# Two PSUM banks for the last two products, two planner costs, and a new order of all queues, in a one-core attention and Fourier-mixing kernel

## The chip, the cores and the metric

The kernel runs on one core of one Trainium2 chip. A core has five engines that run side by side: TensorE (PE in the profile, with its weight loads as PEld), VectorE (DVE), ScalarE (ACT), GpSimd (POOL) and SyncE (SP). SP issues DMAs only; POOL and ACT issue DMAs beside their own work. The metric is the time of one execution on the device in microseconds; lower is better.

## The reference, cut to what matters

Queries, keys and values have 4 batches, 8 heads, 768 positions and 64 elements a head. Attention is local (96 positions back) with 8 global keys and a bias that falls with distance. Its output, per batch 768 x 512, goes through a Fourier mixing and a two-layer network:

```python
scores = scale * np.matmul(q, k.transpose(0, 1, 3, 2)) + bias      # only where local or global
a = softmax(scores); x = np.matmul(a, v)                            # (B, S, H*D)
mixed = np.real(np.fft.fft(np.fft.fft(x, axis=1), axis=2))
u = x + mixed
un = (u - mean(u)) / np.sqrt(var(u) + 1e-06)
return u + np.maximum(un @ w_ch1, 0.0) @ w_ch2                      # 512 -> 2048 -> 512
```

## The kernel before

All work is written down as small units for PE and small operations for the other engines, and then emitted in an order that is written out by hand, one string for each engine (`ORDER` in class `Plan`). PE's units have a letter for their stream and a number in it:

- A: attention. Turning queries and keys (`trans`), scores (`score`), and probabilities times values (`av`). A45 to A60 are batch 2, A61 to A76 batch 3; A61 is the first score of batch 3, of head pair 12 (pairs are counted through the batches, four to each).
- M: mixing. Products with Fourier tables (`y_unit`, `u_unit`) and the turning of the normalised rows for the first three chunks (`nt_unit`). M16 makes chunk 3, M17 is a table product.
- H: the hidden layer. A chunk is 256 of the 3072 rows, there are 12 of them (0 to 11), and for most chunks eight units `ph_unit` make its hidden values, each from one quarter of w1. H24 is the first unit of chunk 3.
- G: the second layer. For each chunk five units, for the last one (chunk 11, `tail`) six: G55 `p1`, G56 `p45`, G57 `p6`, G58 `half(1)`, G59 `p7`, G60 `half(0)`. Chunk sums save one product in eight (lines 1663 to 1676).

An operation on another engine has the name of the unit that it belongs to with a number behind the dot: A10.0 is the first operation that follows A10, here Vector's division of its result; M16.1 and M16.2 make the normalised rows `un` of chunk 3. Operations that belong to no unit begin with T. Those that come up below:

- T.55, T.56: GpSimd loads two quarters of w1. T.84, T.99: GpSimd copies a mirrored piece of a table product. T.85, T.88, T.124 to T.126, T.172 to T.175: GpSimd copies of values (`v_back`, tile vB). T.92: gather of rows of x of batch 1. T.107, T.112, T.117, T.122: loads of values of batch 2. T.110, T.111, T.119, T.152 to T.155, T.160, T.162, T.163, T.165: loads of queries or keys of one head. M7.17, M12.8: GpSimd's inverse deviations of a chunk (`rstd`).
- T.89, T.90: Scalar's queue writes the two halves of x of batch 1 to DRAM; T.91: SP reads them back.
- T.100, T.101, T.102: SP's DMA transposes of `un` to `unT` of chunks 3, 4 and 5. T.136, T.177, T.182, T.185: SP's DMA transposes of queries or keys of a head pair (T.177: the keys of pair 12). T.205, T.206, T.216, T.217, T.267 to T.269: SP stores results.
- T.209: Vector makes a chunk sum for the second layer. T.77, T.78: Vector's steps of the first batch's fold.

PE runs its units strictly in the written order, and so does each of the other engines with its operations; a late operand holds up everything behind it on that engine. Semaphores are set by the tile framework from the program's reads and writes of tiles. GpSimd's DMAs go to a queue of their own (q0 in the profile), SP's to q1, ACT's to q10; all run on the same 16 DMA engines.

PSUM has eight banks. In the last stage four of them serve the rings `ph` and `pg` (two each); `xx` has the other four (two pairs). A unit names the rings that it may take a bank from, and the plan takes the one that comes free first. In the last chunk G58 and G60 both write into the bank that `p45` took for G56 (tile pgD), one into its upper and one into its lower half. The plan counts the two Vector operations that read them before it calls the bank free:

```python
            D_ = GP[c, "D"] = bank(ring, f"pgD_{c}")
            if tail:
                ring.n = 2
```

The plan's costs (the second number of an entry in `pl.later`) only choose among free banks and set the sequence in which the engines' streams are merged while the program is written out; they are no waits on the chip.

Of the kernel before, what the change touches and what calls it, by code (L numbers as in the profile page):

```python
# [17 lines left out]
class Ring(str):  # L18
# [3 lines left out]
    e = 0.0  # L22


class Plan:
# [214 lines left out]
    def unit_start(self, unit):  # L240
# [7 lines left out]
        if not there:  # L248
# [22 lines left out]
        ),  # L271
        "ACT": (
# [11 lines left out]
        ),  # L284
        "DVE": (
# [13 lines left out]
        ),  # L299
        "POOL": (  # L300
# [5 lines left out]
        ),  # L306
        "SP": (
            "T.6 T.0 T.9 T.127 T.35 T.10 T.133 T.128 T.134 T.206 T.136 T.91 T.130 T.137 T.205 T.100 T.131 T.101 T.176 T.177 T.185 T.182 T.102 T.216 T.34 "
            "T.217 T.140 T.186 T.223 T.183 T.222 T.179 T.149 T.180 T.276 T.150 T.151 T.189 T.233 T.234 T.240 T.239 T.198 T.199 T.200 T.257 T.250 T.256 "
            "T.251 T.269 T.267 T.268 "  # L310
# [73 lines left out]
def kernel(  # L384
# [11 lines left out]
    nc = tc.nc  # L396
# [72 lines left out]
    pl = Plan()  # L469
# [178 lines left out]
    def RA(b):  # L648
        return 2 if b else 0
# [168 lines left out]
    def v_back(b, hp):  # L818
        h = slice(2 * hp, 2 * hp + 2)

        def head(r):
            return v16[b % 2][r, h, 0:1, :].to_broadcast([r.stop - r.start, 2, NS - 2, 66])
        after = VN(b, [hp]) + [("sets",)] + [("avh", b - 1, hp)] * (b > 0)
        rows = (slice(0, 32),)

        def cp(eng):
            eng.tensor_copy(vB[hp], v16[b % 2][:, h, 1:NS - 1, :])  # L827
            for r in rows:
                eng.tensor_copy(vB[hp][r], head(r))
        pl.later([("POOL", 0.6 + 0.6 * len(rows), lambda: cp(nc.gpsimd)), ("DVE", 0.3 + 0.3 * len(rows), lambda: cp(V))], after, 0.0, [("vB", b, hp)], rank=RA(b))  # L830
# [473 lines left out]
    def centre(c):  # L1304
# [26 lines left out]
        pl.later([("POOL", 0.82, rstd)], [("ss", c, 0), ("ss", c, 1)], 0.0, [("rstd", c)], rank=2)  # L1331
# [358 lines left out]
    def pg_units(c):  # L1690
# [6 lines left out]
        def prod(o, lhs, rhs, first, last=True):  # L1697
            for j in range(NK):
                nc.tensor.matmul(o, lhs(j), rhs(j), start=(first and j == 0), stop=(j == NK - 1), skip_group_check=True)  # L1699
# [27 lines left out]
        def p45(start, ring):  # L1727
            D_ = GP[c, "D"] = bank(ring, f"pgD_{c}")
            GP[c, "Dr"] = ring
            if tail:  # L1730
                ring.n = 2
# [45 lines left out]
        def half(x, product):  # L1777
            lo, hi = x * HC, (x + 1) * HC

            def run(start, ring):  # L1780
                D_ = GP[c, "D"]
                product(D_[:, lo:hi])
                e = pl.pe(one_us, start)
                if x == 1:
# [3 lines left out]
                         [("ra", c, 1)], e, [("ob", c, 0, x)], ring=GP[c, "Dr"], rank=0)  # L1788
# [19 lines left out]
        if tail:  # L1808
            PG.append(([("s", c, 4), ("rd", c, 0), ("ord", c)], None, half(0, lambda o: prod(o, a(0, 1), bw(1, 0), True))))
# [204 lines left out]
```

## Time and profile before

| | us |
|---|---|
| three runs | 243.40, 242.51, 245.43 |
| median | 243.4 |
| the profiled execution, its own time | 245.22 |
| its span, first to last instruction | 243.4 |
| TensorE busy in it | 231.1 |
| mean granted TensorE clock | 0.990 |

The span is what the profile's numbers are measured in; the profiled execution took 1.8 us more than its span. Times in the profile count from the span's start. In a row of a timeline the columns are the start, the duration, the engine, the line, the operation, what it writes and reads, the shape and the count; in brackets at the end stands how long the engine was idle before it and who ended that. "SPq" and "ACTq" are DMAs that SP and ACT issue. A row of waits gives the engine and line that waited, whom it waited for, the sum of it, how often, and the longest.

### The profile page before, as it was taken

To read this page: it belongs to the slowest core of one execution; us is meant where nothing else is said; L and a number is where in the kernel's file an instruction comes from. 1 tells how busy PE (TensorE), PEld (TensorE's weight loads), DVE (VectorE), ACT (ScalarE), POOL (GpSimd) and SP (SyncE) were. 2 spreads that over 40 slices of the span, in tenths; PEclk is the share of its full clock that TensorE was granted. 3 is DMA by queue.
4 is the path that set the end of the run, shared out by engine and by line. 5 is a ranking of instruction groups with operands and counts; after the bars stand their busy time and mean duration, and the time that the engine had idled before them with its cause. 6 is when DMAs were issued, how large, how long until landed. Compare 5 with 4: busy or idle time off the path is not lost.

```text
span 243.4 us, 7339 instructions
## 1 busy us (share of the span) xinstructions
PE 231.1 (95%) x3074; PEld 193.7 (80%) x3074; DVE 201.5 (83%) x461; ACT 158.3 (65%) x255; POOL 111.9 (46%) x155
## 2 busy tenths in 40 slices
PE   7699899989999996999999999999999999999992
PEld 3366676588988885789888888898889899888881
DVE  3357896989996888489999898999896899898992
ACT  2299599997868855682456877643957677377400
POOL 8998964878440628887026713510070430000220
PEclk9999999999999998899999999999999999999998
DMA  7999999999999999999999695617576272100413
GB/s 184 168 164 175 195 224 207 197 197 174 126 155 181 147 214 119 156 149 108 156 317 246 105 109 149 148 21 202 170 142 164 57 161 54 36 0 4 172 57 118
DMA packets 103249, 35.46 MB, mean 146 GB/s; under 512 B 91088, under 2 KB 98640, under 8 KB 103216
## 3 DMA queue, kind: packets, MB, share of 16 engines
q0 software_dynamic: 72448, 19.16, 79.2%
q1 hardware_dynamic: 27216, 13.08, 27.0%
q10 hardware_dynamic: 3552, 2.75, 4.4%
q8 instruction: 24, 0.39, 0.7%
q14 instruction: 9, 0.07, 0.1%
HBM read 31.44 MB, written 8.65 MB: 165 GB/s over the span
## 4 chain that ended last, share of the span: by engine, by line
PE 81%; ACT 6%; DVE 5%; DMA 5%; issue 1%; ACTq 0%; DVEq 0%
PE ph L1378 23%; PE pgD L1699 16%; PE pgA L1699 12%; PE phA L1471 4%; PE pav L856 4%; PE py L1139 4%; PE phX L1471 3%; PE pu L1226 3%; DMA unT<-un 3%; DMA u<-in_k_dram 3%; ACT ex L800 2%; PE pt L680 2%; PE sc L771 2%; PE sc L739 2%; PE sc L763 2%; PE pf L1047 2%
## 5 line engine op out<-in xcount | busy, mean ns | idle before, releaser
L1378 PE MATMUL ph<-unT,w 128*128 128x256 f16 x576 | 71.3, 275 | 1.9 <-DMA unT<-un 1.8
L1378 PEld LDWEIGHTS <-w 128*128 128x128 f16 x576 | 55.6, 99 | 9.7 <-DMA unT<-un 2.0
L1383 ACT ACTIVATE hT<-ph 128x512 f16<-128x512 f32 x69 | 40.6, 596 | 30.0 <-PE ph L1378 29.6
L1699 PEld LDWEIGHTS <-hT 128*128 128x128 f16 x352 | 34.0, 98 | 4.0
L1329 POOL TENSOR_SCALAR sm<-sm 128x2 f32<-128x2 f32 x12 | 3.6, 301 | 64.2 <-ACT un L1322 62.3
L797 ACT ACTIVATE er<-sc 128x1024 f16<-128x1024 f32 (+1 forms) x24 | 22.3, 952 | 10.7 <-PE sc L771 8.4
L800 ACT ACTIVATE ex<-sc 128x1024 f16<-128x1024 f32 (+1 forms) x24 | 21.8, 971 | 3.1 <-PE sc L739 3.0
L1717 DVE SCALAR_TENSOR_TENSOR u<-pgA,sm,u 128x256 f32<-128x256 f32 (+1 forms) x36 | 20.4, 566 | 2.5 <-PE pgA L1699 1.9
L1717 DVE SCALAR_TENSOR_TENSOR u<-pgD,sm,u 128x512 f32<-128x512 f32 (+1 forms) x25 | 18.0, 724 | 4.9 <-PE pgD L1699 4.6
L812 DVE TENSOR_TENSOR ex<-er,mk 128x1024 f16<-128x1024 f16 (+1 forms) x24 | 16.3, 689 | 5.2 <-ACT er L797 5.1
L868 DVE TENSOR_TENSOR x<-pav,rc 128x384 f16<-128x384 f32 x32 | 16.7, 553 | 0.7
L1322 ACT ACTIVATE un<-un 128x512 f16<-128x512 f16 x24 | 15.0, 626 | 2.5 <-DMA unT<-un 2.5
L856 PEld LDWEIGHTS <-ex 128*128 128x128 f16 x352 | 13.3, 99 | 3.2 <-issue 1.8
L856 PE MATMUL pav<-v,ex 128*128 128x65 f16 x224 | 13.9, 196 | 1.5 <-DVE x L868 0.9
L569 POOL DMA_DIRECT2D qk<-in_q_dram x16 | 13.6, 859 | 1.2 <-PE pt L680 0.7
L921 POOL DMA_INDIRECT xr<-xd,back x3 | 3.5, 1151 | 22.9 <-DVE ex L812 11.7
L569 POOL DMA_DIRECT2D qk<-in_k_dram x16 | 13.6, 860 | 0.1
L1699 PEld LDWEIGHTS <-sb 128*128 128x128 f16 x128 | 12.2, 98 | 1.7
L1568 POOL DMA_INDIRECT out_dram<-u,back x4 | 4.7, 1180 | 17.0 <-DVE u L1717 16.5
L827 POOL COPY vB<-v 128x528 f16<-128x528 f16 x14 | 9.5, 681 | 5.6 <-DMA v<-in_v_dram 4.6
L1152 ACT ACTIVATE zy<-py 128x1024 f16<-128x1024 f32 (+1 forms) x12 | 10.5, 881 | 2.0 <-PE py L1139 1.5
L1699 PE MATMUL pgD<-tt,hT 128*128 128x256 f16 x88 | 11.4, 273 | 0.0
(209 smaller groups left out, 561.8 us busy)
## 6 DMA issues: line engine op xcount, KB each, us to landing
w<-in_moe_w_ch_dram POOLq DMA_DIRECT2D x8, 512.0 KB, 13.9
out_dram<-u SPq DMA_DIRECT2D x15, 256.0 KB, 5.2
v<-in_v_dram POOLq DMA_DIRECT2D x16, 192.0 KB, 7.7
qk<-in_q_dram POOLq DMA_DIRECT2D x16, 96.0 KB, 5.2
qk<-in_k_dram POOLq DMA_DIRECT2D x16, 96.0 KB, 6.3
xr<-xd SPq DMA_DIRECT2D x3, 512.0 KB, 5.3
xd<-x ACTq DMA_DIRECT2D x2, 768.0 KB, 3.8
ex<-w POOLq DMA_DIRECT2D x3, 512.0 KB, 5.9
```

Source lines behind the costliest of these rows:

```text
L569: nc.gpsimd.dma_start(qk16[n][:, w, :, h], src[b, h0 + h].rearrange("(i m) d -> m i d", m=P))
L797: A(mine(), cut(pa), AF.Exp, 0.0, 0.125)
L800: A(cut(expst[hp][:, :, g * 512:g * 512 + (384 if g == 2 else 512)]), cut(pa), AF.Exp, 0.0, 0.125)
L812: VT(o, mine(), m, op=ALU.mult)
L856: nc.tensor.matmul(o[:, s * 65:(s + 1) * 65], lhsT, w, start=(a == 0), stop=(a == len(ops) - 1), skip_group_check=True)
L868: VT(X[b][:, 3 * (k.start + h):3 * (k.start + h) + 3, 2 * hp * Dh:(2 * hp + 2) * Dh].rearrange("p y (h d) -> p y h d", d=Dh), pv[:, h, :, ...
L1322: A(x, x, AF.Square, accum_out=MV[c][:, a, 2:3])
L1378: nc.tensor.matmul(ph[:, a * CH:(a + 1) * CH].rearrange("p (x m) -> p x m", x=2), W1[0][:, d, jb * P:(jb + 1) * P], UNT[c][:, :, d, :], st ...
L1383: pl.later([("ACT", act(512), lambda: A(dst, ph, AF.Relu)), ("DVE", dve(512), lambda: V.tensor_scalar_max(dst, ph, 0.0))], [], e, [("h", c ...
L1471: nc.tensor.matmul(oo.rearrange("p (x m) -> p x m", m=P) if two else oo, lhs(NF * jp + a, d), rhs[:, d], start=(first and a == 0 and d == ...
L1699: nc.tensor.matmul(o, lhs(j), rhs(j), start=(first and j == 0), stop=(j == NK - 1), skip_group_check=True)
L1717: V.scalar_tensor_tensor(o, x, r(t), acc, op0=ALU.mult, op1=ALU.add)
```

## The change

Three things.

The last product, G60 (`half(0)`), takes a bank of its own from `pg` or `ph` (tile pgE) in place of the lower half of pgD. G58 still uses pgD.

```diff
         def p45(start, ring):
             D_ = GP[c, "D"] = bank(ring, f"pgD_{c}")
             GP[c, "Dr"] = ring
-            if tail:
-                ring.n = 2
...
             def run(start, ring):
-                D_ = GP[c, "D"]
+                D_ = GP[c, "D"] if x else bank(ring, f"pgE_{c}")
                 product(D_[:, lo:hi])
...
                 pl.later([("DVE", dve(HC), lambda: stt(u(0)[:, lo:hi], D_[:, lo:hi], 0, u(0)[:, lo:hi]))],
-                         [("ra", c, 1)], e, [("ob", c, 0, x)], ring=GP[c, "Dr"], rank=0)
+                         [("ra", c, 1)], e, [("ob", c, 0, x)], ring=GP[c, "Dr"] if x else ring, rank=0)
...
-            PG.append(([("s", c, 4), ("rd", c, 0), ("ord", c)], None, half(0, lambda o: prod(o, a(0, 1), bw(1, 0), True))))
+            PG.append(([("s", c, 4), ("rd", c, 0), ("ord", c)], ("pg", "ph"), half(0, lambda o: prod(o, a(0, 1), bw(1, 0), True))))
```

Two costs of the plan are raised: that of GpSimd's copy of values and that of its inverse deviation. The instructions stay the same.

```diff
-        pl.later([("POOL", 0.6 + 0.6 * len(rows), lambda: cp(nc.gpsimd)), ("DVE", 0.3 + 0.3 * len(rows), lambda: cp(V))], after, 0.0, [("vB", b, hp)], rank=RA(b))
+        pl.later([("POOL", 0.75 + 0.75 * len(rows), lambda: cp(nc.gpsimd)), ("DVE", 0.3 + 0.3 * len(rows), lambda: cp(V))], after, 0.0, [("vB", b, hp)], rank=RA(b))
...
-        pl.later([("POOL", 0.82, rstd)], [("ss", c, 0), ("ss", c, 1)], 0.0, [("rstd", c)], rank=2)
+        pl.later([("POOL", 1.0, rstd)], [("ss", c, 0), ("ss", c, 1)], 0.0, [("rstd", c)], rank=2)
```

All five strings of `ORDER` are new. PE has the same 284 units, GpSimd the same 114 operations and SP the same 52. Nine operations go from Vector to Scalar (T.72, M0.0, M3.1, M26.0, H20.0, H42.0, H85.1, H92.1, H108.1) and eight from Scalar to Vector (A6.1, M7.10, M7.12, M8.1, H16.0, H19.0, H43.0, H89.1). Most entries move by one to a few places. The stretches that matter here, one string's part to a line:

```diff
 PE, around A10
-A3 A7 A15 A9 A8 A10 A6 A19 A11 A18 A16 A17 A12 A20 A13 A14 A30 A21 A23 A22
+A3 A8 A15 A9 A10 A7 A6 A20 A19 A11 A18 A16 A17 A13 A14 A12 A30 A21 A23 A22
 PE, around H24
-A53 A51 G7 G6 A45 M16 G8 H21 H18 M17 H23 G10 H22 G9 A56 A54 H24 A57 H29 H31 A52 H26
+G7 A53 A51 G6 M16 A45 H21 G8 H18 M17 H23 H22 A56 G9 A54 A52 G10 H24 H26 A57 H29 H31
 DVE, around A21.0
-A15.0 A10.0 A6.0 A11.0 A16.0 T.70 A17.0 T.75 T.76 T.77 T.78 A21.0
+A15.0 A6.1 A10.0 A6.0 A11.0 T.70 A16.0 A17.0 T.75 T.71 T.76 A21.0
 DVE, around M16.2
-A46.1 T.210 A47.1 H17.0 H20.0 G7.0 A53.1 A51.1 G6.0 M16.0 G8.0 M16.2 T.209 A45.1
+A47.1 H17.0 A46.1 T.209 G7.0 T.210 A53.1 M16.0 G6.0 A51.1 G8.0 M16.2 A45.1
 DVE, around M19.2
-M19.0 G14.0 G13.0 A58.0 T.218 M19.2 T.221 A59.0 M19.1
+M19.0 G14.0 M19.1 G13.0 M19.2 A58.0 T.218 A59.0
 ACT, around T.90
-H14.0 M13.0 T.89 M12.7 M12.6 H9.0 M14.0 T.37 T.90 T.40 M15.0 H13.0
+M13.0 H14.0 M7.15 H12.0 H13.0 T.90 M14.0 T.89 M7.16 M15.0
 POOL, around T.55
-T.57 T.65 T.63 T.54 T.61 T.55 T.56 T.114 T.84 T.62 T.85 T.87
+T.54 T.27 T.87 T.63 T.61 T.57 T.65 T.84 T.85 T.55 T.56 T.86 T.88 T.64 T.62
 POOL, from T.108 on
-T.108 T.121 M7.17 T.117 T.119 T.92 T.111 T.110 T.107 T.99 T.122 T.152 M12.8 T.170 T.112 T.169 T.168 T.126 T.211 T.124 T.153 T.154
-T.160 T.157 T.167 T.164 T.155 M16.5 T.125 T.171 T.162 T.163 T.165
+T.108 T.117 T.119 T.121 M7.17 T.92 T.111 T.110 T.107 T.99 M12.8 T.122 T.153 T.152 T.112 T.211 T.126 T.169 T.124 T.168 T.164 T.167
+T.157 T.162 T.125 T.170 T.154 T.155 T.171 T.163 T.165 M16.5
 SP, from T.100 on
-T.100 T.131 T.101 T.176 T.177 T.185 T.182 T.102 T.216 T.34 T.217 T.140
+T.100 T.131 T.101 T.176 T.177 T.102 T.217 T.216 T.185 T.34 T.182 T.140
 SP, at the end
-T.269 T.267 T.268
+T.267 T.269 T.268
```

More of the change, by code (lines that the diff above doesn't have):

```diff
@@ L262 @@
         "PE": (
[8 rows of a table removed]
[8 rows of a table added]
         ),
         "ACT": (
[11 rows of a table removed]
[11 rows of a table added]
         ),
         "DVE": (
[13 rows of a table removed]
[13 rows of a table added]
         ),
         "POOL": (
[5 rows of a table removed]
[5 rows of a table added]
         ),
         "SP": (
-            "T.6 T.0 T.9 T.127 T.35 T.10 T.133 T.128 T.134 T.206 T.136 T.91 T.130 T.137 T.205 T.100 T.131 T.101 T.176 T.177 T.185 T.182 T.102 T.216 T.34 "
-            "T.217 T.140 T.186 T.223 T.183 T.222 T.179 T.149 T.180 T.276 T.150 T.151 T.189 T.233 T.234 T.240 T.239 T.198 T.199 T.200 T.257 T.250 T.256 "
-            "T.251 T.269 T.267 T.268 "
+            "T.6 T.0 T.9 T.127 T.35 T.133 T.128 T.10 T.134 T.206 T.136 T.91 T.130 T.137 T.205 T.100 T.131 T.101 T.176 T.177 T.102 T.217 T.216 T.185 T.34 "
+            "T.182 T.140 T.186 T.223 T.183 T.222 T.179 T.149 T.180 T.276 T.150 T.151 T.234 T.189 T.233 T.240 T.239 T.198 T.199 T.200 T.257 T.256 T.250 "
+            "T.251 T.267 T.269 T.268 "
         ),
```

74 rows, old and new, of the table ORDER are left out of this document.

## Prediction

> **What bounds the kernel now.** I read the page's shares first, then TensorE's (PE's) list of waits, then the table by windows, and the timelines last.
>
> ```profile
> PE 231.1 (95%) x3074; PEld 193.7 (80%) x3074; DVE 201.5 (83%) x461; ACT 158.3 (65%) x255; POOL 111.9 (46%) x155
> ...
> PE   7699899989999996999999999999999999999992
> ...
> PEclk9999999999999998899999999999999999999998
> ...
> PE 81%; ACT 6%; DVE 5%; DMA 5%; issue 1%; ACTq 0%; DVEq 0%
> ```
>
> TensorE works in 231.1 of 243.4 us, so all idle time on it together is 12.3 us, and most of that lies in the first two slices and in the last one. A new order can win only the rest. The one dent far from the ends is slice 16 (the 6), with two slices of a lower clock from there on. The list of PE's waits gives it a name:
>
> ```profile
> PE ph L1378 <- DMA unT<-un: 1.8, 1, 1.8
> ...
> PE pav L856 <- DVE x L868: 0.9, 1, 0.9
> ...
> PE ptu L1351 <- ACT un L1313: 0.5, 1, 0.5
> ```
>
> ```profile
> 90.00:96.00 6.00, 4.15 (x67) 3.34 (x66) 5.86 (x21) 3.43 (x5) 5.84 (x8) 0.95 1.74 129
> 96.00:102.00 6.00, 6.00 (x76) 4.79 (x74) 2.04 (x5) 3.22 (x7) 4.43 (x8) 0.77 2.11 155
> ```
>
> The wait of 1.85 us is followed by a clock of 0.95 and 0.77: 0.05 x 6 + 0.23 x 6 = 1.68 us of TensorE time lost. From 102 us to the end of the products no PE wait is over 0.1 us. So the kernel is bound by TensorE's work, and this change can touch four things: the early waits, this wait with its slow clock, the tail, and whatever new wait the new queues bring.
>
> **The tail (half, p45: two banks).**
>
> ```profile
> 237.05 1.03 PE L1699 MATMUL pgD<-w,mk 128*128 128x256 f16 x8
> 237.92 1.04 PE L1699 MATMUL pgD<-w,zy 128*128 128x256 f16 x8
> 238.39 0.33 SPq L1819 DMA_DIRECT2D out_dram<-u  x1
> 239.00 0.88 DVE L1717 SCALAR_TENSOR_TENSOR u<-pgD,sm,u 128x256 f32<-128x256 f32 x2 [1.12 <-PE pgD L1699]
> 239.51 0.81 SPq L1813 DMA_DIRECT2D out_dram<-u  x2
> ```
>
> G58 (upper half) starts at 237.05 and G60 (lower half) at 237.92, but Vector's two reads of pgD stand one behind the other from 239.00: the first waits for the second product too, since both write one tile. With G60 in a bank of its own (pgE), the first read can go at 237.05 + 1.03 + 0.05 = 238.1 and is done by 238.6, while G60 still runs. The second starts at 239.0 as now and ends at 239.44 instead of 239.88. Its store follows as now. Gain: one read, 0.88 / 2 = 0.44; SP now sends the first half's store ahead of the row that went at 238.39, which costs nothing unless that row lands last: **0.4**. Below by 0 (if the read still waited), above by 0.44.
>
> **The early queues.** A6.1 (one evacuation of turned queries and keys) goes from Scalar to Vector, ahead of A10.0:
>
> ```profile
> 17.71 1.51 ACT L707 ACTIVATE qkT<-pt 128x1536 f16<-128x1536 f16 x1
> ```
>
> ```profile
> 14.82 0.96 DVE L704 COPY qkT<-pt 128x1536 f16<-128x1536 f16 x1 [1.29 <-PE pt L680]
> ...
> 19.25 0.26 DVE L711 COPY mk<-qkT 128x384 f16<-128x384 f16 x1 [1.64 <-ACT qkT L707]
> ...
> 23.93 0.60 DVE L1014 TENSOR_SCALAR zy<-ww 128x128 f16<-128x128 f16 x2
> ```
>
> Scalar gets 1.51 us, Vector pays 0.96 before A10.0, and A11 on PE waits for A10.0's read of the same tile. Vector's idle 1.64 at 19.25 takes that in, and T.77 and T.78 (from 23.93 to 24.7) go behind A21.0, whose read is what the 0.9 us of PE wait ends on. I count nothing: the ends are 0.9 won and 1.0 lost. The 0.5 at ptu stays, as Scalar has the same work ahead of M7.4.
>
> On GpSimd the loads of two quarters of w1 (T.55, T.56) fall behind T.84, which waits for a copy of Vector's until 40.5, and behind a vB copy:
>
> ```profile
> 33.90 0.75 POOL L1891 DMA_DIRECT2D w<-in_moe_w_ch_dram  x1 [0.23 <-DMA v<-in_v_dram]
> ...
> 40.53 0.19 POOL L1173 COPY rev<-zy 128x2 f16<-128x2 f16 x1 [3.40 <-DVE zy L1154]
> ```
>
> ```profile
> w<-in_moe_w_ch_dram POOLq DMA_DIRECT2D x8, 512.0 KB, 13.9
> ```
>
> They go out at about 43 instead of 34. Their queue is full (13.9 us from issue to landing), and the loads ahead of them carry the same bytes in another sequence, so they land when they land now, well before H3 and H4 (54 to 56 us). Cost 0; if the queue ran dry it is up to 43 + 13.9 - 54 = 3 us.
>
> **The wait before H24.** H24 is the first hidden product of chunk 3 and needs the transposed unT that SP issues as T.100.
>
> ```profile
> 88.39 1.23 SPq L1336 DMA_TRANSPOSE unT<-un  x1
> ...
> 92.40 0.60 PE L771 MATMUL sc<-qkT 64*32 64x128 f16 x36
> ...
> 94.85 1.42 PE L1378 MATMUL ph<-unT,w 128*128 128x256 f16 x8 [1.85 <-DMA unT<-un]
> ```
>
> ```profile
> DMA to landing us min/median/max: 3.0/3.2/6.4
> ```
>
> ```profile
> q0 software_dynamic: 988, 0.13, 247.0%
> ```
>
> The transpose took 6.4 us where the median of its kind is 3.2. The last row is the DMA view of 89.7 to 90.5 us: GpSimd's queue q0 alone moves, SP's queue has no packet, though the transpose was issued at 88.39. So GpSimd's loads push it back. Those loads were issued late, after the gather T.92:
>
> ```profile
> 65.88 0.64 POOL L1329 TENSOR_SCALAR sm<-sm 128x2 f32<-128x2 f32 x1 [3.39 <-ACT un L1322]
> ...
> 67.58 1.08 POOL L545 DMA_DIRECT2D v<-in_v_dram  x1
> 68.67 0.84 POOL L569 DMA_DIRECT2D qk<-in_q_dram  x1
> 80.44 1.25 POOL L921 DMA_INDIRECT xr<-xd,back  x1 [10.93 <-PE ph L1378]
> 81.68 1.75 POOL L569 DMA_DIRECT2D qk<-in_k_dram  x2
> 83.33 1.11 POOL L545 DMA_DIRECT2D v<-in_v_dram  x1
> ```
>
> In the new order T.117 and T.119 (67.58, 68.67) stand ahead of M7.17 (65.88, held 3.39 by Scalar), so they leave some 5 us sooner and no longer run beside Scalar's second write of x; SP's T.136 gets its keys sooner; the read T.91 and the gather T.92 follow by an estimated 2 to 3 us sooner, and the three loads behind T.92 with them. They are then over when T.100 goes out (88.4 to 88.7; Vector has T.209 and G6.0 ahead of M16.2 now, so it is no sooner). At the median, 3.2, unT lands at 91.9, and PE comes to H24 at 93.0 plus A52, moved ahead of it, 0.4. The wait goes: **-1.85**, and the slow clock with it: **-1.68**. Bounds: nothing, or all 3.5.
>
> The Trainium skill, "TensorE: Matmul & The Clock Gate", Part 1, has the clock halve after an idle window of about 3.4 us that runs free. The trace agrees on the half clock but not on the length: 1.85 us of idle were enough here. By that rule a new wait of 2 us would cost its own length only; by the row it may cost 1.7 more.
>
> **What is late next.** Past H24 PE is 3.5 us ahead of this trace, and GpSimd is not. A61, the first score of batch 3, needs T.177, the transposed keys of pair 12:
>
> ```profile
> 98.07 0.62 POOL L827 COPY vB<-v 128x528 f16<-128x528 f16 x1 [1.18 <-DMA v<-in_v_dram]
> ...
> 106.07 1.69 POOL L569 DMA_DIRECT2D qk<-in_k_dram  x2
> ...
> 109.57 0.61 POOL L827 COPY vB<-v 128x528 f16<-128x528 f16 x1
> 110.24 0.62 POOL L829 COPY vB<-v 32x528 f16<-32x528 f16 x1
> ```
>
> ```profile
> 113.32 1.21 SPq L658 DMA_TRANSPOSE qkT<-qk  x1
> ```
>
> ```profile
> qkT<-qk SPq DMA_TRANSPOSE x2, 6.5
> ```
>
> ```profile
> 122.05 0.58 PE L771 MATMUL sc<-qkT 64*32 64x256 f16 x36
> ```
>
> SP's row at 113.32 is T.177; the view of 113.3 to 115.3 has such transposes landing 6.5 us after issue, so at 119.8, 2.2 ahead of A61. In the new order PE is there at 122.05 - 3.53 = 118.5. On GpSimd the last load of pair 12 (T.155, the second of the row at 106.07) now has the vB copy T.125 (0.61 + 0.62) ahead of it; T.162 ahead of it replaces T.160. The load is 1.2 later, but one load less (T.162) is left behind it to hold T.177 up, some 0.85. So T.177 lands at 119.8 + 0.4 = 120.2, and PE waits 120.2 - 118.5 = **+1.7**. If the whole 1.2 stays and the copy T.126 waits longer than its 1.18, it is 3 or more; if q0 is emptier, 0. SP's T.185 and T.182 fall behind two stores, but their keys are due after 139 us; T.102 gains from M19.1 and M19.2 going ahead of A58.0.
>
> **The sum**, against the profiled execution's own time, 245.2 (span 243.4 and 1.8 around it): 245.2 - 0.4 - 1.85 - 1.68 + 1.7 = 243.0. That execution lies 1.8 above the median of the runs shown, 243.4, close to the slowest, 245.43; I take it that the slow clock is in it and not in the median run. Against that: 243.4 - 0.4 - 1.85 + 1.7 = 242.85. I say **242.8**, 0.2% less. No change below 2% can be told here.
>
> **The rivals.** (1) A61 is not late: q0 is emptier at 113 to 118, T.177 lands by 118.5. Then 243.4 - 0.4 - 1.85 = 241.15. For it: fewer loads behind T.155; against it: the copy T.125 ahead of it.
>
> The Trainium skill, "DMA: Bandwidth & Descriptors", Queues, rings and completion order, has each DMA engine take turns between queues packet by packet; by that T.177 would not be starved, which is this rival and its 241.15. The row of q0 alone at 89.7 speaks against it.
>
> (2) Slower: GpSimd's chain to T.155 slips more. T.122, the load that T.126 waits for, now goes behind M12.8 (1.3 us), so T.126 waits longer, T.155 ends 2.5 later and A61 waits 3.0, with the slow clock after it, 1.7: 243.4 - 0.4 - 1.85 + 4.7 = 245.85. It decides from a wait of 2.25, where the gains are used up. For it: the 1.18 and 3.39 us that copies wait for loads now; against it: M12.8 stood between the same loads before.
>
> (3) The change does not do what it says: T.91 and T.92 still come late (Scalar writes x's second half after M14.0, as now), q0 holds T.100 up again, the wait stays: 243.4 - 0.4 = 243.0, and A61 is not late.
>
> **How the numbers follow.** Forecast 0.38, rival (1) 0.27, (2) 0.20, (3) 0.15. The range goes from (1) with half of the early 0.9 us, 240.7, to (2) with rounding, 246.0. Outside: more of the early waits gone, or a late w1 (3 us). Faster by over 2% is below 238.5: it needs every wait gone, 0.04. Slower by over 2% is above 248.3: (2) and a late w1 together, 0.05. Within: 0.91.
>
> **What would show it.** Right: Vector's two last reads apart, the first near 238 minus the shift; no wait at the first ph of chunk 3 near 93; q0's loads over by 88; a PE wait at sc L771 <- DMA qkT near 118 to 121. Wrong: a wait on w at 54 to 57, an ACT or DVE wait between 145 and 160 where Vector is near full, or no new wait at all with less than 241.

## The result, and the profile after

After: **242.1 us** median (240.96 to 244.58, 22 runs); before, beside it, 243.2 (242.20 to 245.43, 22 runs). The ratio is 0.995, 95% interval 0.992 to 0.997: about 0.5% less, below the 2% at which a change is called faster. Runs over 1.5% above the fastest of their kernel (here the one of 244.58) count in the medians but not in the ratios and their intervals, and a ratio can differ from the quotient of the medians by up to 0.3%. The profiled execution of after took 242.63 us with a span of 240.8; that of before 245.22 with 243.4. Those two lie 2.6 us apart and the medians 1.0, so the first task is to find which of the 2.6 belongs to the change.

The page of after, with the rows that answer to those of before (busy time, then the 40 slices of PE and of its clock):

```profile
span 240.8 us, 7333 instructions
PE 228.8 (95%) x3074; PEld 192.8 (80%) x3074; DVE 203.5 (85%) x459; ACT 159.6 (66%) x257; POOL 112.4 (47%) x155
...
PE   7879899989999999999999989999999999999993
...
PEclk9999999999999999999999999999999999999998
```

The dent in slice 16 is gone, and the two slices of lower clock with it. There is a small new dent in slice 24. PE's list of waits in after says what is there instead (who waited, for whom; total, times, longest):

```profile
PE sc L739 <- DVE mk L712: 1.5, 1, 1.5
...
PE pav L856 <- DVE x L868: 1.2, 2, 0.7
...
PE sc L771 <- DVE u L1292: 0.9, 1, 0.9
```

No wait for unT, none for the transposed keys of A61. Two waits were not in the list of before at this length: 1.5 us in the start-up (A8, at 14.4 us; before's wait on the same line is 0.2) and 0.9 us (A72, at 139.8, a score of batch 3, in a stretch in which the execution of before had no PE wait above 0.1). Run 10 and the last section come back to both: other executions of before's order have them too.

To compare executions that begin differently, I cut each profile where PE starts certain units. Lengths in us, from the units' first products in thirteen profiles, those of all runs but run 3 (the last column is from the start of the last product, G60, to the end of the span; the span is read to 0.1 us, so this column holds to 0.05):

```
order of                      to M17  M17-A48  A61-A72  A72-H51  G60-end
before: the one shown          87.28    14.86    19.88    11.97     5.48
before: b_again                87.25    12.37    19.88    12.33     5.53
before: b_tail                 87.33    12.86    19.88    12.90     5.03
before: b_tail2                88.30    12.22    19.88    11.91     4.99
before, loads moved: b_pool    87.55    11.24    19.88    13.10     5.53
before, both edits: b_both     87.36    11.24    19.88    12.56     5.00
after                          87.80    11.22    20.80    11.89     5.23
after: a_onebank               87.96    11.22    20.90    11.91     6.04
after: a_start                 87.88    11.22    20.42    11.89     5.22
after: a_sp                    87.00    11.22    20.81    11.89     4.91
after: a_t155                  89.07    11.22    19.88    11.89     5.16
after: c_store                 87.90    11.22    19.88    11.89     4.93
after: c_all                   87.69    11.22    19.88    11.89     4.94
```

The stretch from M17 to A48 holds H24. After is 2.6 us shorter than the execution of before that was shown: +0.5 to M17, -3.6 around H24, +0.9 before A72, -0.1 from A72 to H51, -0.1 in the two stretches left out here (A48 to A61 and H51 to G60) together, and -0.25 at the end.

### The profile page after: what moved, and what is told of

The parts are those of the page before. It is cut to its first block, busy times and chain, and to the rows that moved or that the text cites. A ratio compares the mean times of both kernels' runs of the same rounds, so it can differ in the third digit from the quotient of the medians.

```text
span 240.8 us, 7333 instructions
## 1 busy us (share of the span) xinstructions
PE 228.8 (95%) x3074; PEld 192.8 (80%) x3074; DVE 203.5 (85%) x459; ACT 159.6 (66%) x257; POOL 112.4 (47%) x155
## 4 chain that ended last, share of the span: by engine, by line
PE 81%; DVE 8%; ACT 5%; DMA 3%; issue 1%; DVEq 0%; ACTq 0%
PE ph L1378 24%; PE pgD L1699 16%; PE pgA L1699 12%; PE phA L1471 4%; PE pav L856 4%; PE phX L1471 3%; DMA out_dram<-u 3%; PE py L1139 3%; PE pu L1226 3%; PE sc L771 3%; PE pz L1861 2%; PE pt L680 2%; ACT ex L800 2%; PE sc L739 2%; ACT qkT L707 1%; PE sc L763 1%
## 5 line engine op out<-in xcount | busy, mean ns | idle before, releaser
L1378 PE MATMUL ph<-unT,w 128*128 128x256 f16 x576 | 70.2, 273 | 0.1
L1378 PEld LDWEIGHTS <-w 128*128 128x128 f16 x576 | 55.0, 98 | 7.1 <-issue 0.2
L1383 ACT ACTIVATE hT<-ph 128x512 f16<-128x512 f32 x68 | 40.0, 598 | 23.7 <-PE ph L1378 19.4
L1568 POOL DMA_INDIRECT out_dram<-u,back x4 | 6.2, 1547 | 19.8 <-DVE u L1717 19.2
L856 PEld LDWEIGHTS <-ex 128*128 128x128 f16 x352 | 12.6, 97 | 2.9 <-issue 1.7
L856 PE MATMUL pav<-v,ex 128*128 128x65 f16 x224 | 13.0, 193 | 1.8 <-DVE x L868 1.2
L1152 ACT ACTIVATE zy<-py 128x1024 f16<-128x1024 f32 (+1 forms) x13 | 11.4, 892 | 4.2 <-PE py L1139 4.1
L1699 PE MATMUL pgA<-w,hT 128*128 128x256 f16 x88 | 11.4, 273 | 0.0
## 6 DMA issues: line engine op xcount, KB each, us to landing
w<-in_moe_w_ch_dram POOLq DMA_DIRECT2D x8, 512.0 KB, 10.5
```

The source lines that it names most:

```text
L856: nc.tensor.matmul(o[:, s * 65:(s + 1) * 65], lhsT, w, start=(a == 0), stop=(a == len(ops) - 1), skip_group_check=True)
L1378: nc.tensor.matmul(ph[:, a * CH:(a + 1) * CH].rearrange("p (x m) -> p x m", x=2), W1[0][:, d, jb * P:(jb + 1) * P], UNT[c][:, :, d, :], st ...
L1383: pl.later([("ACT", act(512), lambda: A(dst, ph, AF.Relu)), ("DVE", dve(512), lambda: V.tensor_scalar_max(dst, ph, 0.0))], [], e, [("h", c ...
```

## The experiments

In all comparisons, times are medians in us, beside runs of before on the same chip (243.15 to 243.24 in median).

**1. Before once more (b_again).** No edit.

> The kernel before, unchanged, for one more profile of it. Theory (the wait before H24 belongs to the order, its size and the half clock behind it to the execution): a wait of 1.3 to 2.0 us before H24, with 5.6 us from H24 to A48 where no half clock follows and 7.3 us where it does. Rival (the wait was an accident of the execution shown): under 0.5 us.

Measured: 242.86 us in one execution, span 241.1.

```profile
PE ph L1378 <- DMA unT<-un: 1.1, 1, 1.1
```

```profile
96.00:102.00 6.00, 6.00 (x105) 4.89 (x104) 3.76 (x6) 4.97 (x9) 5.61 (x8) 1.00 1.68 169
```

The wait is there, but it is 1.06 us (row of 1.1), and the clock stays whole (1.00, where the row of before showed 0.77). It is below what the theory allowed (1.3). In the four profiles of this order the stretch M17 to A48 costs 1.0, 1.1, 1.6 and 3.6 us more than the 11.24 that it takes without a wait; in b_tail2 there is no wait for unT, but one of 0.8 us for Vector at A54, just ahead of H24, and unT lands 0.05 us before H24 starts. So a loss here belongs to the order (three of the four wait for unT, 1.06, 1.55 and 1.85 us) and the half clock to one execution in four. Against b_again the profile of after is only 0.3 us shorter.

**2. The loads alone (b_pool).** Before, with one edit on GpSimd:

```
-  ... T.121 M7.17 T.117 T.119 T.92 ...
+  ... T.121 T.117 T.119 M7.17 T.92 ...
```

> Before, with two weight loads of GpSimd (T.117, T.119) ahead of the normalisation M7.17 instead of behind it, nothing else. Theory (the transposed load before H24 was late because these and the later loads were late): they are issued 5 us earlier, unT lands 1 us earlier, the wait before H24 falls from 1.85 to 0.7 us, and the half clock behind it goes; time 0.8 to 1.2 us under before. Rival (the wait went in after because tensor work was put ahead of H24 and the start-up came later): the wait stays at 1.5 us or more and the time within 0.3 us of before.

Measured: 242.03, ratio 0.995 (0.991 to 0.9985). The timeline of GpSimd, then of PE:

```profile
61.93 1.07 POOL L545 DMA_DIRECT2D v<-in_v_dram  x1
62.93 0.88 POOL L569 DMA_DIRECT2D qk<-in_q_dram  x1
...
76.98 1.50 POOL L921 DMA_INDIRECT xr<-xd,back  x1 [9.08 <-PE pgA L1699]
```

```profile
93.20 1.05 PE L1378 MATMUL ph<-unT,w 128*128 128x256 f16 x8
```

The two loads go out at 61.9 and 62.9 instead of 67.6 and 68.7; the gather follows at 77.0 instead of 80.4; and H24 (second fence) has no idle time noted behind it. Two names moved on one queue take away the whole wait, more than the 1.1 us that I expected, and no tensor work was put ahead of H24 here. The rival falls. (T.117 and T.119 load values and queries; "weight loads" in the expectation is a slip, as it is in that of run 4.)

**3. The same loads late in the new order (a_late).** After, with the edit undone: `T.108 T.121 M7.17 T.117 T.119` in place of `T.108 T.117 T.119 T.121 M7.17`.

> After, with the normalisation M7.17 again ahead of T.117 and T.119, so that these two go out 11 us later, at 74.9 and 75.9 us. Theory (the loads' place is what removed the wait before H24): SyncE's transposes from T.136 on are late by 4 to 5 us, unT lands at 95 or later, a wait of 1 us or more before H24 is back; time 1 to 3 us over after. Rival (SyncE's idle 7.8 us before T.100 takes it up): T.100 is issued at 88.8 as in after, wait before H24 under 0.5 us, time within 0.3 us of after.

Measured: 245.54, ratio 1.010 (1.005 to 1.014): 1.0% more than before, clear of the scatter. The profiled execution took 251.28 us, 5.7 over the median, and the other three 244.24 to 245.94; so only single waits and transfers are read from it, no sums:

```profile
PE sc L771 <- DMA qkT<-qk: 2.4, 1, 2.4
...
PE ph L1378 <- ACT hT L1383: 1.8, 1, 1.8
```

```profile
96.00:102.00 6.00, 5.72 (x99) 4.75 (x98) 5.87 (x21) 4.81 (x8) 5.52 (x9) 1.00 1.42 136
127.00:131.00 4.00, 4.00 (x62) 2.70 (x70) 0.00 (x0) 3.21 (x7) 3.13 (x5) 0.57 1.16 349
```

```profile
118.44 1.71 SPq L658 DMA_TRANSPOSE qkT<-qk  x1
...
126.92 0.58 PE L771 MATMUL sc<-qkT 64*32 64x256 f16 x36 [2.38 <-DMA qkT<-qk]
```

The wait came back, but one unit ahead of where I put it: before H22, since Scalar stood 3.2 us in front of chunk 3's normalisation (M16.1), whose rows were late, and H22's bank was behind that. What I had not written down for it is the second wait: A61's, 2.38 us, for the transposed keys issued at 118.44, and behind it the half clock (0.57). That is the wait that the forecast put into after, with the clock of its slower rival behind it, but it comes about in another way: the two loads go out at 77.7 and 78.8 us here, ten us later than in before, and T.177 6.1 us later than in after, of which this execution had lost 2.9 by M17.

**4. The way to A61 made longer (a_t155).** After, with two later loads in front of T.154 and T.155 on GpSimd: `T.170 T.171 T.163 T.154 T.155` in place of `T.170 T.154 T.155 T.171 T.163`.

> After, with two later weight loads (T.171, T.163) ahead of T.154 and T.155 on GpSimd, so that the loads which A61's transposed rows wait for stand two places further back. Theory (the forecast's mechanism holds and only its size failed; slack in after 1.3 us): T.155 is issued 2.0 us and lands 3.0 to 3.7 us later, T.177 lands near 121, TensorE waits 2 to 2.4 us before A61, and the half clock may follow; time 2 to 4 us over after. Rival (the chain from T.155 to A61 is no chain): no wait at A61, time as after.

Measured: 241.98, ratio 0.997 (0.993 to 1.001); no wait at A61. In after the rows are these, with the DMA view of two moments (issue of T.155 and issue of T.177; the last column is us from issue to landing):

```profile
112.32 1.21 SPq L658 DMA_TRANSPOSE qkT<-qk  x1
...
118.95 0.51 PE L771 MATMUL sc<-qkT 64*32 64x256 f16 x23
```

```profile
qk<-in_k_dram POOLq DMA_DIRECT2D x2, 96.0 KB, 3.2
```

```profile
qkT<-qk SPq DMA_TRANSPOSE x1, 5.3
```

and in a_t155:

```profile
116.84 1.25 SPq L658 DMA_TRANSPOSE qkT<-qk  x1
...
120.22 0.58 PE L771 MATMUL sc<-qkT 64*32 64x256 f16 x36
```

```profile
qkT<-qk SPq DMA_TRANSPOSE x1, 3.2
```

T.177 goes out 4.5 us later than in after, 1.3 of it because this execution lost 1.3 us in its start-up, and lands 2.4 later: with nothing left behind it on GpSimd's queue it takes 3.2 us and not 5.3. It lands at 120.1, 0.1 ahead of A61: of the 1.3 us to spare in after, 1.2 are used up. The lost start-up has no part in that, since it made PE and GpSimd's loads late alike (T.170 by 1.28 us, A61 by 1.27). The row of 3.2 in after is the median of T.154 and T.155; T.155 alone took 3.35 us there and 4.68 here. Both theories missed: the chain is there, since T.177 moved, but a transfer that is issued later found less ahead of it.

**5. The tail alone, twice (b_tail, b_tail2).** The order of before with the change's new bank for G60.

```
-  D_ = GP[c, "D"]
+  D_ = GP[c, "D"] if x else bank(ring, f"pgE_{c}")
```

> The order of before with the two-bank tail alone. Theory (the tail and the order are independent): from the last product's start to the end of the span 5.2 us in place of 5.5, so 0.3 us or 0.1% less than before (ratio 0.999), and the wait before H24 stays at 1.5 us or more. Rival (the tail is worth what the forecast said): 0.4 us less. Second rival (the whole gain of 1.0 us sits in the tail): ratio 0.996.

Measured: 241.93, ratio 0.995 (0.992 to 0.998); G60 to the end 5.03 us where before has 5.48 to 5.53. That is 0.5 and not the 0.3 of the theory, nearer to the rival's 0.4; the wait before H24 stayed (1.55). The profile gives 0.5, the median 1.3, so it was run again:

> The order of before with the two-bank tail again, since the first comparison gave 1.3 us where its profile showed 0.5 us between the last product and the end. Theory (0.5 us is the tail, the rest the scatter of the runs): 0.3 to 0.8 us under before, a wait of 1.3 us or more before H24, 5.0 us from G60 to the end. Rival (the tail is worth more than its profile shows): 1.1 us or more under before again.

Measured: 242.59, ratio 0.997 (0.994 to 1.000), with 4.99 to the end; the median is 0.6 us under before, the ratio says 0.75. The wait of 1.3 us before H24 didn't come (0.8 at A54, see run 1). Both profiles show 0.5 us for the tail. That the rest of the first figure was scatter is likely, not shown: the interval of the first ratio ends at 0.6 us.

**6. The new order without the tail (a_onebank).** After, with both last products in pgD.

> The order of after with the one-bank tail of before. Theory: the order alone carries the gain: no wait before H24, no wait before A61, the wait of 0.85 us before A72 there again, about 0.7 us less than before (ratio 0.997), and 5.5 us from the last product's start to the end. Rival (the order does nothing for the median, the tail everything): ratio 1.000.

Measured: 243.11, ratio 1.002 (0.998 to 1.005). The order alone brings nothing that can be measured. Its H24 stretch is as short as in after, so the loss must be elsewhere; the end shows a part of it:

```profile
236.94 0.88 DVE L1717 SCALAR_TENSOR_TENSOR u<-pgD,sm,u 128x256 f32<-128x256 f32 x2 [1.12 <-PE pgD L1699]
237.45 0.33 SPq L1813 DMA_DIRECT2D out_dram<-u  x1
237.82 0.43 SPq L1819 DMA_DIRECT2D out_dram<-u  x1
238.35 0.40 SPq L1813 DMA_DIRECT2D out_dram<-u  x1
```

The new order of SyncE has T.267 (line 1813), which needs Vector's late read, ahead of T.269 (line 1819), whose data Vector has finished 1.1 us before that read begins (235.06 + 0.75, in the same timeline). With one bank this makes it 6.04 us from G60 to the end in place of 5.5. Order and tail are not independent, as I had assumed.

**7. SyncE's stores in after (a_sp).** `T.251 T.269 T.267 T.268` in place of `T.251 T.267 T.269 T.268`.

> After, with SyncE's third store from the end (T.269) ahead of T.267, as before has it. Theory (T.269's data is ready 0.75 us before T.267's, and it stands behind it in after): it goes out at 235.6 in place of 236.7, the last store of all 0.2 us sooner, from G60 to the end 5.0 us in place of 5.2; time 0.2 us under after, which one comparison of medians can't tell from nothing. Rival (the last landing follows the last read alone): 5.2 us.

Measured: 241.28, ratio 0.994 (0.991 to 0.997). The end of after and then of a_sp:

```profile
235.57 1.04 PE L1699 MATMUL pgE<-w,zy 128*128 128x256 f16 x8
235.77 0.48 DVE L1717 SCALAR_TENSOR_TENSOR u<-pgD,sm,u 128x256 f32<-128x256 f32 x1 [0.25 <-PE pgD L1699]
236.28 0.33 SPq L1811 DMA_DIRECT2D out_dram<-u  x1
236.64 0.48 DVE L1717 SCALAR_TENSOR_TENSOR u<-pgE,sm,u 128x256 f32<-128x256 f32 x1 [0.39 <-PE pgE L1699]
236.66 0.43 SPq L1817 DMA_DIRECT2D out_dram<-u  x1
237.19 0.39 SPq L1811 DMA_DIRECT2D out_dram<-u  x1
```

```profile
234.79 1.04 PE L1699 MATMUL pgE<-w,zy 128*128 128x256 f16 x8
...
235.26 0.33 SPq L1817 DMA_DIRECT2D out_dram<-u  x1
235.64 1.07 SPq L1811 DMA_DIRECT2D out_dram<-u  x2
```

Counted from G60, T.269 goes out at 0.47 in place of 1.09, and the end comes at 4.91 in place of 5.23. The 0.3 is the stores' order: the three profiles of the new order with two banks and T.267 first have 5.16 to 5.23 us here, the three with T.269 first 4.91 to 4.94. Of the median's 0.85 under after no more than that is shown to be its work.

**8. Both edits on before (b_both).** The edits of 2 and 5 together, nothing else of the new order.

> Before, with two edits alone: the two-bank tail, and T.117 and T.119 ahead of M7.17. Theory (these two carry the whole gain, the rest of the new order is worth nothing): no wait before H24, TensorE at the last product G60 at 235.4 us as with the load move alone, 5.0 us from there to the end as with the tail alone, span 240.4 us, median 241.5 us, at or under after. Rival (the other changes of the order carry a part of the gain): 242.5 us or more.

Measured: 241.62, ratio 0.995 (0.992 to 0.998), the same as after; span 239.9, no wait before H24, 5.00 to the end, G60 at 234.90 us. Two names moved on one queue and one bank do all that the new order of five queues does, as far as intervals of 0.3% either way can tell. They can't tell the tail's 0.5 us apart either: the loads alone (run 2) have the same ratio.

**9. The start-up put back (a_start).** After, with every queue of before up to unit A14, and A6.1 on Scalar.

> After, with the start-up order of before on all engines up to about 20 us. The copies of 128x384 in front of A8 take 0.3 us again. Theory (a loss there is absorbed later): TensorE is 0.5 to 0.7 us ahead at A22 and a wait of 0.3 us before H24 comes back, and the wait before A72 grows by what is left; time within 0.3 us of after. Rival (a start-up loss passes to the end in full): 0.5 to 0.7 us under after, 241.5 where after has 242.1.

Measured: 242.52, ratio 0.998 (0.995 to 1.001). No wait before H24 came back, and nothing passed to the end. The copy of 128x384 took 1.36 us and not the 0.3 expected. The waits before A8 and A11 are gone, and PE is 0.7 us sooner at A22, in spite of a clock of 0.64 from 12 to 16 us in this execution; but the way from M0 to M2 is 0.8 us longer than in after (10.0 and 9.2), and by M17 the gain is gone (87.88, after 87.80). Run 11 repeats it.

**10. The wait before A72 (c_store).** As a_sp, and SyncE's store T.222 ahead of the transposed load T.183: `T.223 T.222 T.183 T.179` in place of `T.223 T.183 T.222 T.179`.

> After with two stores moved on SyncE: T.269 ahead of T.267, and the store T.222 ahead of the transposed load T.183. Theory (the wait of 0.85 us before A72 is that of Vector's M22.6 for T.222's landing, and T.222 is slow because it stands behind T.183): T.222 lands 1.5 us or more sooner, M22.6 waits under 1.3 us, the wait before A72 goes, time 0.5 to 0.9 us under after with the first of the two moves alone. Rival (T.222 is slow because GpSimd's loads share the DMA engines): it lands within 0.5 us of 137, the wait before A72 stays at 0.6 us or more, no gain.

Measured: **241.28**, ratio 0.992 (0.9895 to 0.995). In after, Vector's M22.6 stood idle for a store that reads the same buffer (last line: us from issue to landing):

```profile
L1817 SPq DMA_DIRECT2D out_dram<-u x1: 342/342/342, 129.9 to 129.9; - x1
...
  DMA out_dram<-u: 2.8, 1
...
DMA to landing us min/median/max: 7.6/7.6/7.6
```

and in c_store:

```profile
L1817 SPq DMA_DIRECT2D out_dram<-u x1: 337/337/337, 130.0 to 130.0; - x1
...
DMA to landing us min/median/max: 3.8/3.8/3.8
```

Issued at the same time, it lands in half, Vector's wait is gone, and A61 to A72 takes 19.88 us again.

The wait is not the new order's own. T.183 stands ahead of T.222 in before too, and in three of the six profiles with PE's order of before (b_tail, b_pool, b_both) Vector stands idle for such a store for 2.1 to 2.4 us, and PE has the same wait one score later, before A68: 0.83, 0.64 and 0.48 us. It is in the stretch A72 to H51 of the table. In b_tail:

```profile
PE sc L771 <- DVE u L1292: 0.8, 1, 0.8
```

The theory's mechanism holds; its gain doesn't show in the median, which equals a_sp's: this execution had lost 0.9 us more than a_sp's by M17, and has made it up by G60 (234.77 and 234.79).

**11. All together (c_all).** c_store with the start-up of before.

> As the kernel with the two stores moved, and the start-up order of before on all engines. Theory (a start-up gain passes to the end only as far as no later wait takes it): TensorE 0.5 us sooner at M17 where the clock is whole, no wait before H24 (unT lands 0.3 us or more before it), and at most 0.5 us less in all. Rival (the wait before A72 or H24 takes it): the same time as without the start-up order.

Measured: 241.34, ratio 0.995 (0.992 to 0.998). PE is 0.2 us sooner at M17 and at G60 than in c_store, with a wait of 0.4 in front of A26 (35 us), where a_start has 0.3: M0 to M2 takes 10.0 us again, and the gain is lost there. M17 comes anywhere from 87.00 to 87.96 in four profiles with one and the same start-up order, so no gain of the start-up can be told. c_store and a_sp are under both kernels in median; by their intervals they are told apart from before, not from after or from each other.

## Why the prediction was right, and where its steps were not

The forecast was 242.8; 242.1 was measured, within the range. Against the medians beside them the forecast said 0.6 less and 1.0 was measured. But that the sum came so near is in part luck: two of its terms were off in opposite directions.

- **Tail, -0.4.** Right in size: 0.5 by itself (b_tail, b_tail2), 0.25 to 0.3 in after, because the step "SP now sends the first half's store ahead of the row that went at 238.39, which costs nothing" failed. It costs 0.3 (a_sp).
- **The wait before H24, -1.85, and the half clock, -1.68.** The mechanism was right, down to the two loads (b_pool, a_late). T.117 and T.119 went out 4.9 us sooner and T.92 2.4, as forecast (5; 2 to 3). But the size was that of one execution: the stretch loses 1.0 to 1.6 us in the three others. And the step "at the median, 3.2, unT lands at 91.9" failed: with no other transfer under way at its issue T.100 took 4.8 us in after, landed at 93.67, and H24 started at 93.89, so the wait went with 0.2 us to spare. Taking the half clock out of the median run was right, as none of the three other executions has it.
- **The new wait at A61, +1.7.** This term failed: 0 in after, with 1.3 us to spare. The step that failed is "T.177 lands at 119.8 + 0.4", for it kept T.155's time to landing: T.155 was issued 2.0 us later than in before (108.91; 106.89), but with the pause of a vB copy ahead of it took 3.35 us to landing in place of 6.38, and T.177 5.3 in place of 6.5. So T.177 landed at 117.7, 2.1 sooner than in before and not 0.4 later. PE's arrival was foreseen right (118.5; 118.95). At this place rival (1) was the true case; its time, 241.15, is too low because it took off the whole 1.85 and had no wait at A72. "DMA: Bandwidth & Descriptors" of the Trainium skill (Queues, rings and completion order) has each DMA engine take turns between the queues packet by packet; the traces show 3.2 us (a_t155), 5.3 (after) and 8.4 (a_late) for T.177, so its time still goes with what the other queues hold.
- **Early queues, 0.** PE is 0.5 us later at M17 in after than in the execution of before that was shown, but executions of one order differ by more (87.00 to 87.96), and putting the start-up order back returned nothing that can be told from that. The 0 stands within it. The longer wait before A8 came from a place that the step hadn't weighed (last section).
- **Not foreseen: A72, +0.9** in that stretch. The step "what is late next" took A61 for the next wait; the next one was that for the store T.222, which frees a buffer and stands behind T.183. It is in before's order too, wherever PE comes there soon enough (run 10), so it is no loss of the new order: before's takes 0.4 to 1.2 us longer in A72 to H51 in four of its six profiles.
- Of the signs named, Vector's two reads stood apart, H24 had no wait, and no wait for w1 came. The wait at L771 for qkT near 118 to 121 didn't come; that was the sign that the forecast's own case had failed.

The Trainium skill, "TensorE: Matmul & The Clock Gate", Part 1, with its idle window of about 3.4 us, would give no half clock in any of these: there was none after 1.55 us (b_tail) and 1.84 us (a_late, H22), and one after 1.85 (before) and 2.38 (a_late, A61). The length of the idle time alone does not part 1.84 from 1.85; where it falls does (first point of the last section).

## What to carry to other kernels

Read a wait in more than one profile before its length goes into a sum: here it was 1.06, 1.55 and 1.85 us in three executions of one order, and absent in a fourth. One and the same transfer (T.177) took 3.2 to 8.4 us to landing, by what the queues held at that moment, so when loads move, work out anew what stands ahead of them. And a queue's order is worth a look wherever a store waits that frees a buffer or ends the kernel: moving one name of SyncE's queue took 0.3 us off the end (a_sp), and two names of GpSimd's brought as much as a new order of all five queues (b_pool and after, both 0.995). And ask what is late next until nothing is: the wait behind the one that was removed was in the old order as well, hidden by it.

## What the runs showed of the hardware

- The granted clock is set in windows of 3.41 us that run free of the kernel. In every trace it changes only at whole multiples of 3.413 us from its first change; in before it goes to full at 6.64 us, to half at 95.38 (26 windows on) and back at 98.80 (one more). Before's wait of 1.85 us lay whole in one window, 91.97 to 95.38, which had PE busy for 1.56 us, and the next window had half the clock; so did the one after the wait of 2.38 us in a_late (1.04 busy). The wait of 1.84 us in a_late was split between two windows with 2.54 and 2.44 us of work, that of 1.55 in b_tail between two with 3.18 and 2.09, and the clock stayed whole. So whether one wait costs 1.7 us more was a matter of where it fell, and the window need not be idle. How little work it takes is not settled: a window with 1.57 us of work at the end of c_store (234.23 to 237.65) was followed by the whole clock.
- Where the transposed load T.183 ran among other transfers, they took longer. With T.183 behind T.222 and not ahead of it, GpSimd's loads of the same stretch took 7.2 to 7.5 us in place of 9.1 to 10.5 from issue to landing, though none of them was moved. The other runs agree: 8.7 to 12.5 us in four more profiles with T.183 ahead, 5.0 to 6.9 in c_all with it behind. Whether a plain load in its place would do the same was not tried. After, then c_store:

```profile
qk<-in_k_dram POOLq DMA_DIRECT2D x2, 96.0 KB, 10.5
v<-in_v_dram POOLq DMA_DIRECT2D x1, 192.0 KB, 9.5
```

```profile
qk<-in_k_dram POOLq DMA_DIRECT2D x2, 96.0 KB, 7.2
v<-in_v_dram POOLq DMA_DIRECT2D x1, 192.0 KB, 7.5
```

- A delay on PE in the start-up need not reach the end: a_t155 is 1.27 us behind after at M17 and 0.37 at G60, since the wait before A72 is for a store's landing and not for PE. That may be a part of why edits that each save some tenths do not add up; no run takes it apart.
- The longer wait before A8 goes with a Vector copy that GpSimd seems to hold up. The two copies ahead of it (128x384 and 128x128) take 0.40 us together in before and b_pool, and 0.5 to 2.1 elsewhere, with either order; with before's order PE waits up to 0.7 us for them (b_both). First b_again, then after:

```profile
12.24 1.19 DVE L711 COPY mk<-qkT 128x384 f16<-128x384 f16 x1
12.62 0.69 POOL L827 COPY vB<-v 128x528 f16<-128x528 f16 x1
13.35 0.17 DVE L712 COPY mk<-qkT 128x128 f16<-128x128 f16 x1
```

```profile
12.23 1.52 DVE L711 COPY mk<-qkT 128x384 f16<-128x384 f16 x1
12.78 0.89 POOL L619 DMA_DIRECT2D qk<-in_q_dram  x1
13.59 0.71 POOL L827 COPY vB<-v 128x528 f16<-128x528 f16 x1
13.68 0.68 DVE L712 COPY mk<-qkT 128x128 f16<-128x128 f16 x1
```

Each slow copy ends within 0.12 us after an instruction of GpSimd: at 13.43 after the copy that ends at 13.31, at 13.75 after the load issue that ends at 13.67, at 14.36 after the copy that ends at 14.30. After puts a load issue and two copies of GpSimd across this place and A8 right behind it. The Trainium skill, "SBUF — State Buffer" (SBUF: two separate sides), names one port pair that GpSimd and Vector's faster copies share, as a lock that whoever starts first holds for a whole instruction. The ends of these rows agree; the starts fit only if a load issue holds the lock too, since in b_again Vector's copy begins at 12.24, within a load issue of GpSimd (11.61 to 12.68) and before GpSimd's copy (12.62). No run took the GpSimd work away, so this is read from the traces and not shown by an experiment.
